# Two transposed weight loads of 640 rows issued as 512 and 128 rows each, with the waits split to match

## The chip, the core and the metric

The kernel runs on one core of one Trainium2 chip. The metric is the device time of one execution in microseconds (us); the span in a profile is some 1.3 us shorter.

## The reference, cut to what matters

Two branches over the same x (2048 x 640) are mixed by a gate.

```python
g = sigmoid((x * gate_w).sum(-1, keepdims=True))
# branch A: a diagonal complex state space model
Bu   = einsum("bld,pd->blp", x, B_bar)          # B_re and B_im, 640 x 640 each
hseq = scan(Lam_bar, Bu)
a    = 2 * einsum("blp,dp->bld", hseq, C).real + x * Dskip
# branch B: a dense layer pair, W1 640 x 1728, W2 1728 x 640
b    = gelu(x @ w1 + b1) @ w2 + b2
out  = g * a + (1 - g) * b
```

The kernel's matmuls take B_re and B_im transposed from SBUF (the on-chip memory), and it loads them with DMA transposes.

## The kernel before

The kernel is a list of operations with dependencies and priorities. A list scheduler in Python fixes each engine's order, and a wait is emitted for each dependency across engines. What matters here is the start. TensorE first multiplies the first quarter of x (512 tokens) by W1, in two parts. The first part (40 products, two of them split in halves) goes block by block as W1's row blocks arrive. The second part has 25 matmuls. Then come the 50 matmuls with B: 25 with B_re and 25 with B_im, five for each 128 rows of B.

```python
WSPLIT = {0: 4, 1: 6, 3: 6}          # W1's row blocks 0, 1 and 3 are loaded in two pieces
...
xtrans(0, range(4, 5), 4.5, 0.8)     # last number but one: priority on SyncE's queue
w1load(4, "sp", 5)                   # W1's fifth row block, 256 KB
...                                  # two more W1 loads (prio 20, 21)
for ci, src in enumerate((A_B_re, A_B_im)):
    load_T(f"B{ci}", f"l_B{ci}", [(BT[:, ci, :, :], src)], [("BT", ci)], prio=30 + ci, dur=4.1)
xtrans(1, range(KD), 32, 3.4)        # x, second quarter, a transpose too
load("gwb", "sp", "l_gwb", gwb[:, :], gate_w.partition_broadcast(128), ["gwb"], prio=32.2)
load("xnb", "sp", ...,     prio=32.4)                # both plain loads
...
def bproj(q):                        # the B product of quarter q
    for ci in range(2):
        for k in range(KP):          # KP = 5 blocks of 128 rows
            def f_mm(...):
                for kd in range(KD):
                    t = nc.tensor.matmul(PS[bank][:, :], BT[:, ci, kd, k * 128:(k + 1) * 128], xT[q][:, kd, :], ...)
            op(f"b_{q}_{k}{ci}", "pe", KD * d_mm(512), XT[q] + [("BT", ci)], [("bank", bank)], f_mm, prio=pe_prio())
```

All these loads are issued by SyncE, one after the other, on one queue. W1's first row block is already loaded in two halves (`WSPLIT`), here and in the changed kernel; the diff does not touch it.

Of the kernel before, what the change touches and what calls it, by code (L numbers as in the profile page):

```python
# [147 lines left out]
class Prog:  # L148
# [8 lines left out]
    def op(self, name, eng, dur, reads, writes, fn, prio=None, lat=0.0, after=()):  # L157
        deps = {}
        for k in reads:
            for w in self.last_w.get(k, ()):  # L160
                deps[w.idx] = w
        for k in writes:
            for w in self.last_w.get(k, ()):
                deps[w.idx] = w
            for r in self.last_r.get(k, ()):
                deps[r.idx] = r
        for a in after:
            deps[a.idx] = a
        deps = list(deps.values())
        E = self.E  # L170

        def run(eg, deps=deps, eng=eng, fn=fn):
            E.wait(eng, *[d.done for d in deps if not (eng == "pe" and d.eng == "pe")])
            return fn()

        it = self.sch.add(name, eng, dur, deps, run, prio=prio, lat=lat)
        for k in writes:
            self.last_w[k] = [it]
            self.last_r[k] = []
        for k in reads:  # L180
            self.last_r.setdefault(k, []).append(it)
        return it


def bass_gated_mix__ssm_conv_s5__dense_activation_gelu__prompt_kernel(
# [18 lines left out]
    _, S, D = A_x.shape  # L204
# [3 lines left out]
    KD = D // 128  # L208
    KP = P // 128
# [16 lines left out]
    with ExitStack() as es:  # L226

        def SB(name, shape, dt):
            return es.enter_context(nc.sbuf_tensor(name, list(shape), dt))
# [5 lines left out]
        BT = SB("BT", [128, 2, KD, P], BF16)  # L235
# [72 lines left out]
        op = pr.op  # L308

        def inc(eng, ins):  # L310
            return E.inc(eng, ins, eng + "_s")

        def dma_inc(eng, ins, sem):
            SEM(sem)
            E.count.setdefault(sem, 0)
            ins.then_inc(sems[sem], 16)
            E.count[sem] += 16
            return (sem, E.count[sem])

        def d_act(n):  # L320
            return 0.26 + n * 0.00084
# [4 lines left out]
        def d_mm(n):  # L326
            return n / 2400.0 + 0.004
# [8 lines left out]
        def load_T(name, sem, pairs, writes, prio, dur, lat=3.0, reads=()):  # L336
            def fn():
                t = None
                for dst, src in pairs:
                    t = dma_inc("sp", nc.sync.dma_start_transpose(dst, src), sem)  # L340
                return t
            return op(name, "sp", dur, reads, writes, fn, prio=prio, lat=lat)
# [10 lines left out]
        def xtrans(q, ks, prio, dur):  # L353
            load_T(f"xT{q}_{ks[0]}", f"l_xT{q}_{ks[0]}", [(xT[q][:, ks[0]:ks[-1] + 1, :], x2[q * 512:(q + 1) * 512, ks[0] * 128:(ks[-1] + 1) * 128])],
                   [("xT", q, k) for k in ks], prio, dur)
# [33 lines left out]
        for i, (nm, (r0, src)) in enumerate(ROWS.items()):  # L389
            src = src.rearrange("(k p) -> k p", p=128)  # L390
# [29 lines left out]
        for i, (k, c0, c1) in enumerate(((0, 0, 2), (0, 2, 4), (1, 0, 2), (1, 2, 4))):  # L420
            bank = (7, 6, 5, 4)[i]
# [18 lines left out]
        XT = {q: [("xT", q, k) for k in range(KD)] for q in range(1, NQ)}  # L440
# [137 lines left out]


        for ci, src in enumerate((A_B_re, A_B_im)):  # L580
            load_T(f"B{ci}", f"l_B{ci}", [(BT[:, ci, :, :], src)], [("BT", ci)], prio=30 + ci, dur=4.1)
        xtrans(1, range(KD), 32, 3.4)
        load("gwb", "sp", "l_gwb", gwb[:, :], gate_w.partition_broadcast(128), ["gwb"], prio=32.2)
        load("xnb", "sp", "l_xnb", xn[0][:, :, KN * 128:D], x2[0:512, KN * 128:D].rearrange("(c p) d -> p c d", p=128),
# [16 lines left out]
        def pe_prio():  # L601
            ctr["pe"] += 1
            return ctr["pe"]


        def next_bank():
            ctr["bank"] += 1
            return (ctr["bank"] - 1) % 8
# [87 lines left out]
        def bproj(q):  # L696
            for ci in range(2):
                for k in range(KP):
                    bank = next_bank()

                    def f_mm(k=k, ci=ci, bank=bank):
                        t = None
                        for kd in range(KD):
                            t = nc.tensor.matmul(PS[bank][:, :], BT[:, ci, kd, k * 128:(k + 1) * 128], xT[q][:, kd, :],  # L704
                                                 start=(kd == 0), stop=(kd == KD - 1))
                        return inc("pe", t)

                    op(f"b_{q}_{k}{ci}", "pe", KD * d_mm(512), XT[q] + [("BT", ci)], [("bank", bank)], f_mm, prio=pe_prio())

                    def f_ev(k=k, ci=ci, bank=bank):  # L710
                        dst = U[q % 2][:, :, ci, k, :]
                        src = PS[bank][:, :].rearrange("p (s t) -> p s t", s=2)
                        return inc("act", nc.scalar.activation(dst, src, ACT.Copy, scale=1.0 if ci == 0 else -1.0))  # L713

                    op(f"u_{q}_{k}{ci}", "act", d_act(512), [("bank", bank)], [("U", q % 2, k, ci)], f_ev, prio=10)
# [292 lines left out]
        m1_first()  # L1008
        m1(0, NW)
        bproj(0)  # L1010
        ssm(0)
        gates(0)
        m1(1)
        for q in range(0, NQ, 2):
            m1_tail(q)
        ssm(1)
        bproj(1)
        ssm(2)
        gates(1)
        outsT(0)  # L1020
        for q in range(2, NQ):
            ssm(2 * q - 1)
            bproj(q)
            ssm(2 * q)
            m1(q)
            xnload(q, "pool")
            gates(q)
            if q < NQ - 1:
                outsT(q - 1)
# [63 lines left out]
```

## Time and profile before

| | before |
|---|---|
| median of 3 runs | 213.42 us (213.19 to 213.48) |
| span of the profiled run | 212.1 us |
| TensorE busy | 208.9 us, 99% |
| first matmul with B | 19.72 us |
| from there to the end | 192.38 us |

The head of the page of the kernel before, and its section on the chain that ended last:

```profile
span 212.1 us, 2749 instructions
PE 208.9 (99%) x1102; PEld 104.9 (49%) x1102; DVE 190.2 (90%) x240; ACT 103.2 (49%) x177; POOL 4.2 (2%) x12
PE 90%; DMA 4%; SPq 4%; issue 0%; DVE 0%
```

TensorE has practically no idle time to give. The chain in order of time (start, duration, what) shows the only stretch of the chain that is a DMA:

```profile
9.87 0.53 SPq L333
10.39 0.04 issue
10.44 9.24 DMA BT<-in_A_B_re_dram
19.68 0.05 issue
19.72 10.97 PE ps L704 x50
30.69 14.03 PE ps L661 x65
```

From 19.72 us on, TensorE alone makes up the chain until 210.17 us. Before that the chain runs through SyncE's issues to B_re's load. The list of TensorE's waits (line, for what, us in total, times, longest) and the timelines of TensorE and of SyncE around that point:

```profile
PE ps L704 <- DMA BT<-in_A_B_re_dram: 0.4, 1, 0.4
```

```profile
13.79 5.56 PE L661 MATMUL ps<-xT,W1sb 128*128 128x512 bf16 x25
19.72 10.97 PE L704 MATMUL ps<-xT,BT 128*128 128x512 bf16 x50 [0.38 <-DMA BT<-in_A_B_re_dram]
```

```profile
10.44 5.35 SPq L340 DMA_TRANSPOSE BT<-in_A_B_re_dram  x1
15.82 4.61 SPq L340 DMA_TRANSPOSE BT<-in_A_B_im_dram  x1
20.48 3.32 SPq L340 DMA_TRANSPOSE xT<-in_A_x_dram  x1
```

The 0.38 us in brackets understates the loss, because a matmul's duration (379 ns) overlaps the next matmul: they start every 0.2155 us. The last W1 matmul started at 18.96 us, so the next could have started at 19.18. The start at 19.72 lost 0.54 us.

A DMA ends with up to sixteen completion events on its semaphore, one for each DMA engine; the Trainium skill says so in "DMA: Bandwidth & Descriptors", section "Why a DMA increments its semaphore by 16 and not by 1", and the trace agrees with sixteen events for each B load. B_re's came in two groups:

```
B_re, kernel before, completion events in us
17.65 17.66 17.68 17.71 17.77 17.80 | 19.56 19.58 19.60 19.61 19.61 19.62 19.62 19.64 19.66 19.68
```

### The profile page before, as it was taken

How to read it: one execution, taken by the hardware profiler on the slowest of the kernel's cores; microseconds unless marked ns; L12 is line 12 of the kernel's file. 1: busy time of each engine (PE TensorE's matmuls, PEld its weight loads, DVE VectorE, ACT ScalarE, POOL GpSimd, SP SyncE). 2: the span in 40 equal slices, each digit the busy share in tenths (PEclk: the TensorE clock that was granted, in tenths of full speed). 3: DMA queues.
4: the chain of work that ended last, by engine and by line, in shares of the span. 5: the costliest groups of instructions: out<-in, count | busy, mean ns of one | idle time of the engine just before them, and what ended most of it. 6: DMA issues, size and time to landing. Idle time of an engine off the chain costs nothing.

```text
span 212.1 us, 2749 instructions
## 1 busy us (share of the span) xinstructions
PE 208.9 (99%) x1102; PEld 104.9 (49%) x1102; DVE 190.2 (90%) x240; ACT 103.2 (49%) x177; POOL 4.2 (2%) x12
## 2 busy tenths in 40 slices
PE   8999999999999999999999999999999999999996
PEld 4443444444564444444464444444446444567775
DVE  2499999999999998999999999899999999499744
ACT  2488556679860253556681063455660027623330
POOL 1000000030000000000000000000010000000000
DMA  5899999998600020066363000007642000005251
GB/s 150 193 289 183 184 206 219 362 191 178 159 0 3 0 49 0 0 105 86 60 58 115 3 0 0 0 2 146 85 93 99 0 3 0 0 0 102 68 142 63
DMA packets 48888, 19.08 MB, mean 90 GB/s; under 512 B 41452, under 2 KB 47980, under 8 KB 48876
## 3 DMA queue, kind: packets, MB, share of 16 engines
q1 hardware_dynamic: 47216, 17.59, 39.7%
q0 software_dynamic: 1600, 1.32, 4.3%
q8 instruction: 8, 0.13, 0.3%
q14 instruction: 4, 0.03, 0.1%
q10 hardware_dynamic: 60, 0.01, 0.0%
HBM read 8.41 MB, written 2.63 MB: 52 GB/s over the span
## 4 chain that ended last, share of the span: by engine, by line
PE 90%; DMA 4%; SPq 4%; issue 0%; DVE 0%
PE ps L704 20%; PE ps L928 20%; PE ps L661 20%; PE ps L977 15%; PE ps L791 7%; PE ps L840 5%; DMA BT<-in_A_B_re_dram 4%; SPq L333 3%; SPq L340 2%; PE ps L682 1%; PE ps L939 1%; PE ps L805 0%; DVE W1sb L874 0%
## 5 line engine op out<-in xcount | busy, mean ns | idle before, releaser
L661 PE MATMUL ps<-xT,W1sb 128*128 128x512 bf16 x220 | 48.1, 379 | 0.0
L744 DVE TENSOR_TENSOR_SCAN W<-atab,V 128x1280 bf16<-128x1280 f32 x16 | 44.3, 2811 | 0.3
L704 PE MATMUL ps<-xT,BT 128*128 128x512 bf16 x200 | 43.8, 379 | 0.4 <-DMA BT<-in_A_B_re_dram 0.4
L928 PE MATMUL ps<-Gl,W2sb 128*128 128x512 bf16 (+1 forms) x234 | 42.7, 344 | 0.0
L668 ACT ACTIVATE Gl<-ps,cols 128x512 bf16<-128x512 f32 x44 | 29.9, 694 | 15.5 <-PE ps L661 15.5
L661 PEld LDWEIGHTS ps<-xT,W1sb 128*128 128x128 bf16 x220 | 21.5, 98 | 26.0
L977 PE MATMUL ps<-Hb,CT 128*128 128x512 bf16 x150 | 32.9, 379 | 0.0
L928 PEld LDWEIGHTS ps<-Gl,W2sb 128*128 128x128 bf16 x234 | 22.9, 98 | 19.3
L713 ACT ACTIVATE U<-ps 128x512 bf16<-128x512 f32 x40 | 23.7, 596 | 16.2 <-PE ps L704 16.1
L704 PEld LDWEIGHTS ps<-xT,BT 128*128 128x128 bf16 x200 | 19.4, 98 | 24.4 <-DMA BT<-in_A_B_re_dram 0.9
L946 ACT ACTIVATE E1T<-ps,cols 128x512 bf16<-128x512 f32 (+1 forms) x18 | 9.5, 624 | 36.0 <-PE ps L939 36.0
L977 PEld LDWEIGHTS ps<-Hb,CT 128*128 128x128 bf16 x150 | 14.4, 98 | 17.9 <-DVE V L496 0.6
L985 ACT ACTIVATE E2T<-ps 128x512 bf16<-128x512 f32 x15 | 9.1, 604 | 13.6 <-PE ps L977 13.6
L791 PE MATMUL ps<-W2sb,Gl 128*128 128x320 bf16 x104 | 14.8, 299 | 0.0
L614 DVE SCALAR_TENSOR_TENSOR trf<-xn,gwb 128x640 bf16<-128x640 bf16 x16 | 13.2, 823 | 0.4
L496 DVE TENSOR_TENSOR Hb<-Hb,V 128x1280 bf16<-128x1280 bf16 x16 | 12.5, 821 | 0.3
L496 DVE TENSOR_TENSOR V<-V,W 128x1280 bf16<-128x1280 bf16 x16 | 12.5, 821 | 0.3
L496 DVE TENSOR_TENSOR V<-mr,U 128x2560 bf16<-128x2560 bf16 x8 | 11.9, 1492 | 0.3
L791 PEld LDWEIGHTS ps<-W2sb,Gl 128*128 128x128 bf16 x104 | 10.1, 98 | 4.3 <-issue 0.3
L496 DVE TENSOR_TENSOR Hb<-c,W 128x2560 bf16<-128x2560 bf16 x8 | 11.9, 1491 | 0.2
L496 DVE TENSOR_TENSOR W<-mi,U 128x2560 bf16<-128x2560 bf16 x8 | 11.9, 1485 | 0.0
L496 DVE TENSOR_TENSOR V<-s,W 128x2560 bf16<-128x2560 bf16 x8 | 11.9, 1484 | 0.0
(91 smaller groups left out, 151.0 us busy)
## 6 DMA issues: line engine op xcount, KB each, us to landing
W2sb<-in_B_w_dram SPq DMA_DIRECT2D x1, 2080.0 KB, 8.7
out_dram<-xn SPq DMA_DIRECT2D x3, 640.0 KB, 4.8
xn<-in_A_x_dram POOLq DMA_DIRECT2D x2, 640.0 KB, 6.8
trf<-grow SPq DMA_DIRECT2D x3, 256.0 KB, 5.0
xn<-in_A_x_dram SPq DMA_DIRECT2D x1, 640.0 KB, 6.9
W1sb<-in_B_w_dram SPq DMA_DIRECT2D x2, 256.0 KB, 3.0
W1sb<-in_B_w_dram SPq DMA_DIRECT2D x1, 480.0 KB, 4.1
out_dram<-W1sb SPq DMA_DIRECT2D x3, 160.0 KB, 1.8
```

The source lines that it names most:

```text
L496: return inc("dve", nc.vector.tensor_tensor(out=o, in0=a, in1=b, op=o_))
L614: t = inc("dve", nc.vector.scalar_tensor_tensor(out=scr[:, :], in0=xn[q % 2][:, c, :], scalar=1.0, in1=gwb[:, :], op0=ALU.mult, op1=ALU.mu ...
L661: t = nc.tensor.matmul(PS[bank][:, :], W1sb[:, k, jf * 128:(jf + 1) * 128], xT[q][:, k, :], start=(k == 0), stop=(k == KD - 1))
L668: return inc("act", nc.scalar.activation(Gl[q % 2][:, jf, :], PS[bank][:, :], ACT.Gelu_apprx_tanh, bias=b1col[:, jf:jf + 1]))
L704: t = nc.tensor.matmul(PS[bank][:, :], BT[:, ci, kd, k * 128:(k + 1) * 128], xT[q][:, kd, :], start=(kd == 0), stop=(kd == KD - 1))
L713: return inc("act", nc.scalar.activation(dst, src, ACT.Copy, scale=1.0 if ci == 0 else -1.0))
L744: t = inc("dve", nc.vector.tensor_tensor_scan(out=g[:, ci, :], data0=a, data1=v[:, ci, :], initial=0.0, op0=ALU.mult, op1=ALU.add))
L791: t = nc.tensor.matmul(PS[bank][:, 0:HALF], Gl[q % 2][:, jf, t4 * 128:(t4 + 1) * 128], W2sb[:, jf, cols], start=False, stop=False, skip_gr ...
L840: t = nc.tensor.matmul(PS[bank][:, 0:n], H[b % NHB][:, ci, k, s * 128:(s + 1) * 128], CT[:, ci, k, cols], start=(i == 0), stop=(i == 2 * K ...
L928: t = nc.tensor.matmul(PS[bank][:, 0:t1 - t0], W2sb[:, jf, d * 128:(d + 1) * 128], Gl[q % 2][:, jf, t0:t1], start=(jf == 0), stop=False)
L946: return inc("act", nc.scalar.activation(E1T[:, d, t0:t1], PS[bank][:, 0:t1 - t0], ACT.Identity, bias=cols2[:, 0, d:d + 1]))
L977: t = nc.tensor.matmul(PS[bank][:, :].rearrange("p (s t) -> p s t", s=2), CT[:, ci, k, d * 128:(d + 1) * 128], Hb[:, 2 * (q % 2):2 * (q % ...
```

## The change

Each B matrix is loaded by two transposes, of 512 rows and of 128 rows. A B product waits only for the part that holds its own 128 rows. The intent is that TensorE can start on the first four row blocks of B_re before the fifth has landed.

```diff
         for ci, src in enumerate((A_B_re, A_B_im)):
-            load_T(f"B{ci}", f"l_B{ci}", [(BT[:, ci, :, :], src)], [("BT", ci)], prio=30 + ci, dur=4.1)
+            for i, (p0, p1) in enumerate(((0, 512), (512, KP * 128))):
+                load_T(f"B{ci}{i}", f"l_B{ci}{i}", [(BT[:, ci, :, p0:p1], src[p0:p1, :])], [("BT", ci, i)], prio=30 + ci + 0.1 * i, dur=0.8 * (p1 - p0) / 128)
...
-                    op(f"b_{q}_{k}{ci}", "pe", KD * d_mm(512), XT[q] + [("BT", ci)], [("bank", bank)], f_mm, prio=pe_prio())
+                    op(f"b_{q}_{k}{ci}", "pe", KD * d_mm(512), XT[q] + [("BT", ci, k // 4)], [("bank", bank)], f_mm, prio=pe_prio())
```

## The prediction

> **What bounds the kernel now.** The page gives TensorE 208.9 us busy of a 212.1 us span (99%). The chain of waits is TensorE at 90%, unbroken from 19.72 us to 210.17 us; ahead of it stand the first loads' issues and one 9.24 us DMA, the transposed load of B_re. The list of TensorE's waits names one on a DMA: 0.4 us for B_re. VectorE (190 us busy) has slack where TensorE needs it: its H for the output products at 72.5, 123.0 and 173.5 us was done at 67.8, 110.4 and 152.9 us.
>
> **The one spot the change touches.** In the timeline SyncE issues the B_re transpose from 10.44 to 15.79 us and B_im from 15.82 to 20.43. B_re's semaphore events in the trace: six of sixteen at 17.65-17.80 us, ten only at 19.56-19.68. TensorE starts its last matmul of the first W1 product at 18.97 us and its first B matmul at 19.72 us. Matmuls of this form follow each other every 0.216 us (50 in 10.79 us), so an unhindered start is 19.19 us: 0.53 us is lost. That is all a faster B_re can give; no engine work is removed.
>
> **What the change adds and moves.** Two transposes of 640 rows become four of 512, 128, 512, 128. Issue times in the trace: 3.32 us for 512x640 (x, second block), 1.12-1.20 us for 512x128. A line through these is about 0.57 us fixed plus 0.137 us per 128x128 block (an estimate): 3.3 + 1.3 = 4.6 us for a split matrix against 5.35 and 4.61 now. Landing ends 1.9 us after the issue ends when nothing delays it, up to 3.9 us with stragglers like B_re's.
> - B_re, 512 rows: issue ends at 13.8-14.8 us, landed at 15.7-18.7 us. Needed at 19.2: the wait goes.
> - B_re, 128 rows: needed 20 matmuls later, 23.5 us; landed by about 20.
> - B_im, 512 rows: landed at 20.3-23.4 us (now 23.12), needed at 24.6.
> - B_im, 128 rows: landed by 24.8, needed at 28.9.
> - x, second block: landed 25.8 us now, perhaps 26-28 then, needed at 30.2.
>
> Later loads have several us of slack.
> The kernel's list scheduler already assumes B there in time, so I expect no new instruction order.
>
> **The risk.** The destination of each transpose becomes strided (512 of 640 columns) where it was contiguous. The Trainium skill, "DMA: Bandwidth & Descriptors", section "Latency and other measured facts", gives 261 GB/s for a transpose with non-contiguous mid-dim against about 350-400 GB/s contiguous. This trace's contiguous ones move 290 GB/s in their bulk, so I expect little loss. And each hand-over from one transpose to the next shows a slow stretch (62-195 GB/s for 1 to 2 us behind B_re and B_im); two more of these could use up the roughly 1.3 us of margin of B_im.
>
> **Prediction.** 213.42 - 0.5 = 212.9 us; the gain is passed on whole because TensorE has no other wait. 80% range 212.5 to 213.5. Faster by over 2%: 0.01; within 2%: 0.97; slower by over 2%: 0.02.
>
> **What the profile would show.** Right: TensorE's 0.4 us wait for B_re gone, first B matmul near 19.2 us, the chain running on TensorE or its W1 loads before that, all later stages shifted by 0.4-0.5 us, unchanged busy times. Wrong: a B issue of 512 rows longer than 4.5 us, a wait of the 26th B matmul on B_im or of the second W1 product on x, or a later stage that doesn't shift since VectorE or a DMA holds it.

## The result, and the profile after

| | before | after |
|---|---|---|
| first measurement, median of 6 runs each | 213.50 us | 213.19 us |
| repeated later (after_again), median of 11 and 5 runs | 213.36 us | 213.05 us |
| span of the profiled run | 212.1 us | 211.7 us |
| last W1 matmul of the first quarter starts | 18.96 us | 19.11 us |
| first matmul with B starts | 19.72 us | 19.33 us |
| from there to the end | 192.38 us | 192.38 us |

The ratio to before was 0.9987 (95% interval 0.9974 to 1.0000), and 0.9980 (0.9963 to 0.9996) in the repetition. A ratio is the mean time of one kernel's runs over that of the other's of the same rounds, so it is not quite the ratio of the medians quoted here. The change is worth 0.1 to 0.2%. The first interval touches 1 and the repetition's stays below it.

The head of the page of the changed kernel and its chain by engine:

```profile
span 211.7 us, 2739 instructions
PE 207.5 (98%) x1088; PEld 104.7 (49%) x1102; DVE 190.1 (90%) x240; ACT 103.0 (49%) x177; POOL 4.2 (2%) x12
PE 93%; SPq 4%; DMA 2%; issue 1%; DVE 0%
```

The lower busy time of TensorE is not less work. The page counts 1,088 matmuls where 1,102 weight loads are recorded: fourteen matmul records are missing from this trace, and some short "issue" gaps of TensorE in it are those holes. The chain in order of time around the start, changed kernel:

```profile
8.77 3.30 DMA W1sb<-in_B_w_dram
12.07 0.14 issue
12.21 1.89 PE ps L640 x8
14.09 5.40 PE ps L662 x25
19.49 3.45 PE ps L705 x16
```

B_re is gone from the chain. What stands there now is the load of W1's fifth row block. The waits of TensorE and the timelines say the same:

```profile
PE ps L640 <- DMA W1sb<-in_B_w_dram: 0.6, 1, 0.6
```

```profile
12.21 1.89 PE L640 MATMUL ps<-xT,W1sb 128*128 128x512 bf16 x8 [0.62 <-DMA W1sb<-in_B_w_dram]
13.93 5.56 PE L662 MATMUL ps<-xT,W1sb 128*128 128x512 bf16 x25
19.33 10.96 PE L705 MATMUL ps<-xT,BT 128*128 128x512 bf16 x49
```

```profile
10.44 6.26 SPq L340 DMA_TRANSPOSE BT<-in_A_B_re_dram  x2
16.74 4.85 SPq L340 DMA_TRANSPOSE BT<-in_A_B_im_dram  x2
21.63 2.92 SPq L340 DMA_TRANSPOSE xT<-in_A_x_dram  x1
```

From 13.93 us the timeline has no bracket: TensorE goes from W1 to B without standing still. The span shrank by 0.4 us, which is the 0.54 us no longer lost at B minus 0.15 us by which the W1 part ended later in this execution. Instruction order on all compute engines is the same as before.

The order of events of the four parts, from the semaphore events (last of sixteen): B_re 512 rows 17.83 us, B_re 128 rows 20.23, B_im 512 rows 22.73, B_im 128 rows 24.03, x second quarter 26.60.

### The profile page after: what moved, and what is told of

Read it like the earlier page. It is cut to its first block, busy times and chain, and to the rows that moved or that the text cites. A ratio compares the mean times of both kernels' runs of the same rounds, so it can differ in the third digit from the quotient of the medians.

```text
span 211.7 us, 2739 instructions
## 1 busy us (share of the span) xinstructions
PE 207.5 (98%) x1088; PEld 104.7 (49%) x1102; DVE 190.1 (90%) x240; ACT 103.0 (49%) x177; POOL 4.2 (2%) x12
## 4 chain that ended last, share of the span: by engine, by line
PE 93%; SPq 4%; DMA 2%; issue 1%; DVE 0%
PE ps L662 22%; PE ps L705 20%; PE ps L929 20%; PE ps L978 15%; PE ps L792 7%; PE ps L841 5%; SPq L333 2%; SPq L340 2%; DMA W1sb<-in_B_w_dram 2%; PE ps L683 1%; PE ps L940 1%; PE ps L640 1%; PE ps L806 0%; DVE W1sb L875 0%
## 5 line engine op out<-in xcount | busy, mean ns | idle before, releaser
L662 PE MATMUL ps<-xT,W1sb 128*128 128x512 bf16 x215 | 47.5, 379 | 0.3
L705 PE MATMUL ps<-xT,BT 128*128 128x512 bf16 x196 | 43.1, 379 | 0.3 <-issue 0.2
L929 PEld LDWEIGHTS ps<-Gl,W2sb 128*128 128x128 bf16 x234 | 22.9, 98 | 19.3
L705 PEld LDWEIGHTS ps<-xT,BT 128*128 128x128 bf16 x200 | 19.5, 98 | 23.8 <-ACT Gt L691 0.4
```

The costliest lines, as they stand in the source:

```text
L662: t = nc.tensor.matmul(PS[bank][:, :], W1sb[:, k, jf * 128:(jf + 1) * 128], xT[q][:, k, :], start=(k == 0), stop=(k == KD - 1))
L929: t = nc.tensor.matmul(PS[bank][:, 0:t1 - t0], W2sb[:, jf, d * 128:(d + 1) * 128], Gl[q % 2][:, jf, t0:t1], start=(jf == 0), stop=False)
```

## The experiments

The explanation read from the two profiles (theory A) is: only the earlier landing of B_re's first rows matters, the transfers are no faster, and afterwards the early W1 loads set the pace. The traces bear out the middle part: all of B_re had landed at 19.68 us before, and only at 20.23 and 19.88 us in the two profiles of the change. Two rivals for *why* the whole B_re landed so late came up as well. Theory H: a second transpose right behind on the same queue holds up the landing. Theory F: a 16 KB instruction fetch, which starts at 17.05 us in the kernel before, holds it up.

"Lost" below is the start of the first B matmul minus that of the last W1 matmul minus 0.2155 us. Span minus first B start is 192.36 to 192.41 us in every profile but those of e6 and e9 (193.01 and 192.71), where B_im comes late. So apart from these, **the start of the first B matmul alone decides the time**. By the same rule a run without a profile tells roughly where its first B matmul started, by its span less 192.37 us: an estimate of 19.1 to 19.9 us over the eleven runs of the change, and 19.4 to 20.6 us over the eleven of the kernel before in the repetition. One profile is one draw from such a range.

| kernel | last W1 mm | first B mm | lost | span | ratio to before (95%) |
|---|---|---|---|---|---|
| before | 18.96 | 19.72 | 0.54 | 212.1 | 1 |
| the change | 19.11 | 19.33 | 0 | 211.7 | 0.9987 (0.9974-1.0000) |
| after_again | 18.95 | 19.16 | 0 | 211.5 | 0.9980 (0.9963-0.9996) |
| e1_re_only | 18.94 | 19.45 | 0.29 | 211.9 | 0.9980 (0.9966-0.9994) |
| e2_wait_both | 19.21 | 20.16 | 0.73 | 212.5 | 0.9998 (0.9978-1.0018) |
| e3_before_fetch | 20.36 | 20.58 | 0 | 212.9 | 1.0037 (1.0021-1.0054) |
| e4_after_w14 | 19.97 | 20.19 | 0 | 212.6 | 0.9990 (0.9973-1.0007) |
| e5_before_w14 | 20.24 | 20.71 | 0.25 | 213.1 | 1.0036 (1.0016-1.0056) |
| e6_before_gap | 19.14 | 19.36 | 0 | 212.4 | 1.0018 (0.9999-1.0037) |
| e7_after_fetch | 20.25 | 20.46 | 0 | 212.8 | 1.0037 (1.0021-1.0053) |
| e8_after_w4split | 19.34 | 19.56 | 0 | 211.9 | 1.0001 (0.9985-1.0017) |
| e9_before_gwb | 19.15 | 19.36 | 0 | 212.1 | 0.9980 (0.9965-0.9995) |
| e10_after_gwb | 19.22 | 19.44 | 0 | 211.8 | 0.9979 (0.9966-0.9992) |
| e11_after_gwb_w4split | 19.20 | 19.42 | 0 | 211.8 | 0.9982 (0.9969-0.9995) |

The profile columns are from one execution each; the ratios are from 5 or 6 timed runs against 6 (the first measurement of the change) or 11 (all others) of the kernel before. All outputs were correct.

### after_again: the change once more

The edit adds nothing. It gives a second profile and more timings.

> The change unaltered, for a second profile and more timings. Ratio 0.997 to 0.9998. If the early W1 loads set its time, the first B matmul starts 0.22 us after the last W1 matmul starts unless the instruction fetch falls into the landing of B_re's first part, in which case it lands near 19.4-20 us and up to 0.5 us are lost again.

Measured: ratio 0.9980, 0 lost. TensorE goes through from W1 to B:

```profile
13.77 5.56 PE L662 MATMUL ps<-xT,W1sb 128*128 128x512 bf16 x25
19.16 10.96 PE L705 MATMUL ps<-xT,BT 128*128 128x512 bf16 x49
```

In this execution there was no wait for W1's fifth block either, so that wait comes and goes.

### e1_re_only: split B_re alone

```diff
-            for i, (p0, p1) in enumerate(((0, 512), (512, KP * 128))):
+            for i, (p0, p1) in enumerate(((0, 512), (512, KP * 128)) if ci == 0 else ((0, KP * 128),)):
...
-    XT[q] + [("BT", ci, k // 4)]
+    XT[q] + [("BT", ci, k // 4 if ci == 0 else 0)]
```

> Only B_re is split in 512 and 128 rows, B_im stays whole. Theory A (the gain is the earlier landing of B_re's first 512 rows alone): B_re's 512 rows land near 17.8 us, TensorE has no wait for B_re, first B matmul near 19.1 us, time like the change's: ratio to before 0.997 to 0.9995. Rival: the split of B_im is needed too, then a wait on B_im appears at the 26th B matmul and the ratio is 0.9995 or more.

Measured: ratio 0.9980, as with the full change: splitting B_im contributes nothing that shows. The profile was worse than expected, though:

```profile
13.76 5.57 PE L662 MATMUL ps<-xT,W1sb 128*128 128x512 bf16 x25
19.45 10.75 PE L705 MATMUL ps<-xT,BT 128*128 128x512 bf16 x49
```

B_re's first 512 rows landed only at 19.40 us, in two groups again, and 0.29 us were lost. B_im landed at 24.76 us, just in time: the weight load of the 26th B matmul started 0.16 us late, but the matmul itself, at 24.86 us, did not. So an early landing of the first part is not assured; the table further below shows when it fails. Even here something was gained: the landing took 3.9 us from the end of the issue, as in the kernel before, but the issue of 512 rows ended 0.28 us sooner than that of 640.

### e2_wait_both: the four transposes, but each product waits for both parts

```diff
-    XT[q] + [("BT", ci, k // 4)]
+    XT[q] + [("BT", ci, 0), ("BT", ci, 1)]
```

> The same four transposes as in the change, but every B product waits for both parts of its matrix. Theory A (the gain is the finer wait, the transfers are no faster): both parts of B_re are there only at about 20.2 us, first B matmul near 20.3 us, about 1.1 us later than with the change and 0.5 us later than before: ratio 1.002 to 1.005. Rival B (four smaller transposes are faster as transfers): no worse than before, ratio 0.9985 to 1.000.

Measured: both parts were there at 20.07 us and the first B matmul started at 20.16, as theory A had it. (The view names "issue" as what ended the wait; the landing is read from the semaphore events.) The last W1 line and the B line of this kernel's timeline:

```profile
14.04 5.56 PE L662 MATMUL ps<-xT,W1sb 128*128 128x512 bf16 x25
20.16 10.09 PE L705 MATMUL ps<-xT,BT 128*128 128x512 bf16 x46 [0.56 <-issue]
```

The ratio, 0.9998 (0.9978 to 1.0018), missed the 1.002 or more expected under theory A and lies in the range given for rival B. It cannot separate the theories: the runs scattered from 212.82 to 214.14 us, the interval also holds the change's 0.9980, and the profiled run was the second slowest of six. By the estimate from spans the fastest run started B at 19.1 us, without a wait. What speaks for theory A is the traces: with the same four transposes and coarse waits, 0.73 us were lost in this profile; with fine waits, none in the two of the change; and all of B_re landed later than before in all three (20.07, 20.23 and 19.88 us). The gain comes from the finer wait, not from faster transfers; how much a coarse wait costs on average these runs do not tell.

### e4_after_w14 and e5_before_w14: W1's fifth block issued earlier

If the W1 loads now set the pace, issuing the late one sooner should help the changed kernel and not the old one. The same edit on the change (e4) and on the kernel before (e5):

```diff
-        w1load(4, "sp", 5)
+        w1load(4, "sp", 4.4)      # ahead of the fifth x transpose (4.5)
```

> The change, and W1's fifth row block is issued ahead of the fifth x transpose instead of behind it. Theory A (with the change the W1 loads, not B, set when the B product starts): the wait of 0.6 us on that block goes, it lands near 10.5 us instead of 12.07, first B matmul near 18.5 us, ratio 0.995 to 0.998. Rival: the B product's start is bound by B_re at 17.8 us or by another early load, no more gain: ratio 0.9985 to 0.9995.

> The kernel before with the same swap of two issues, transposes whole. Theory A: B_re still lands at about 19.7 us, so the first B matmul stays at 19.7 us and the wait for B_re only grows to 0.8-1.2 us: ratio 0.9990 to 1.0010. Rival: the swap is worth as much here as on top of the change, ratio 0.995 to 0.998.

Measured: theory A failed in both. For e4 its rival came true: another early load takes over, ratio 0.9990. For e5 neither range held, since the kernel became slower. The fifth block stopped being late, but the next W1 load, now right behind a transpose, landed at 14.73 us (e4) and 15.01 us (e5) instead of 13.45, and TensorE waited for that one. The start of the second part of the W1 product, e4 first, then e5:

```profile
14.78 5.57 PE L662 MATMUL ps<-xT,W1sb 128*128 128x512 bf16 x25 [1.19 <-DMA W1sb<-in_B_w_dram]
```

```profile
15.06 5.57 PE L661 MATMUL ps<-xT,W1sb 128*128 128x512 bf16 x25 [0.98 <-DMA W1sb<-in_B_w_dram]
```

The swap made the kernel before 0.36% slower; on top of the change it left no gain over before that clears the noise. It moved the wait rather than removing it, and it confirms in the other direction that a later W1 part delays everything behind it.

### e3_before_fetch and e7_after_fetch: 84 instructions more in TensorE's queue

The trace shows eight DMA packets of 16,384 bytes on the instruction queue. The Trainium skill, "Runtime: NRT & Kernel Launch", section "Instruction fetch mechanics", says that a sequencer refills its instruction memory in blocks of 16 KiB, 256 instructions, over a DMA queue of its own. That fits TensorE: the trace lists 2,228 instructions for it (1,102 matmuls, 1,102 weight loads, 24 others), which make 8.7 such blocks. To move the fetch, waits that are already satisfied were put in (the same edit on both kernels). Four for each of 42 matmuls are 168 calls; the traces list 84 more instructions, and nine fetches instead of eight:

```diff
                 def f_mm(jf=jf, k=k, t0=t0, t1=t1):
+                    for _ in range(4):
+                        nc.tensor.wait_ge(sems["pe_s"], 1)
                     return inc("pe", nc.tensor.matmul(...))   # first part of the W1 product
```

> The kernel before, with four waits that are always satisfied ahead of each of the first 42 W1 matmuls (84 more instructions in TensorE's queue), nothing else. In five profiles out of six a 16 KB instruction fetch starts at 16.9 to 18.4 us, and B_re's or its first part's last engines land 1.1 to 1.9 us after the first ones. Theory F (the fetch, TensorE's own, holds B_re up): 84 instructions more bring the fetch forward by some 5 us, to about 11-12 us; B_re lands 1.9 to 2.5 us after its issue ends, so at 17.7-18.3 us instead of 19.7; TensorE's wait for B_re goes, ratio 0.997 to 0.9995 without any split. Theory H (the next transpose, right behind, holds it up): B_re still lands at 19.5-19.9 us, ratio 0.9995 to 1.001. If the extra instructions slow TensorE, the gaps between its first 42 matmuls grow beyond 0.216 us.

> The change, with the same 84 satisfied waits as the other run. Theory F: the first 512 rows of B_re land at 17.3-18 us in this profile too, TensorE doesn't wait for them; the split has then nothing more to give than the moved fetch: ratio to before 0.997 to 0.9995, within 0.1% of the kernel before with the moved fetch. Rival: the split and the moved fetch add up, ratio 0.994 to 0.997.

Measured: the extra instructions cost TensorE 1.3 to 1.4 us in the first part of W1 (its second part starts at 15.19 and 15.07 us, against 13.79), so the times cannot test theory F. Neither ratio, 1.0037 twice, lies in a range that was expected. Two things can still be read. First, the second and third fetches came earlier, 46.29 to 38.62 us and 66.80 to 60.39 us, so they are TensorE's; the first did not move (17.47 us in e3, 1.3 us after the end of B_re's issue, as before). It seems to be held back until a transpose has been read; that was not tested. In e3 B_re landed in two groups again, at 19.70 us.

Second, e3 and e7 are a clean test of the explanation. Here TensorE comes to B at 20.5 us, after B_re's landing (19.70 us whole in e3, 18.72 us for the first part in e7), and the two kernels, one split and one not, have the same ratio, 1.0037. **Where B is not waited for, the split is worth nothing.** The B line of e3, without a wait, and its two B issues:

```profile
20.59 9.66 PE L706 MATMUL ps<-xT,BT 128*128 128x512 bf16 x43
```

```profile
10.43 5.74 SPq L340 DMA_TRANSPOSE BT<-in_A_B_re_dram  x1
16.21 4.08 SPq L340 DMA_TRANSPOSE BT<-in_A_B_im_dram  x1
```

### e6_before_gap and e9_before_gwb: no split, plain loads between the two transposes

e6 moves two plain loads between the whole transposes of B_re and B_im, e9 only the gate row (160 KB):

```diff
-    load("gwb", ..., prio=32.2)
+    load("gwb", ..., prio=30.2)        # e6 and e9
-    load("xnb", ..., prio=32.4)
+    load("xnb", ..., prio=30.4)        # e6 alone
```

> The kernel before, with two plain loads (the gate row and the rest of x's first block) moved between the two B transposes. Theory H: with no transpose right behind it B_re lands within 2.4 us of its issue's end, at 17.7-18.2 us, the wait for it goes: ratio 0.997 to 0.9995 if B_im, about 1 us later, is still in time (24.6 us). Theory F: the fetch at about 17 us still holds B_re up to 19.3-19.9 us: ratio 0.9995 to 1.002.

> The kernel before, with one plain load alone (the gate row, 160 KB) between the whole transposes of B_re and B_im. Theory H (a transpose right behind holds the landing up, a plain load doesn't): B_re lands in one group within 2.4 us of its issue's end, by 18.3 us, TensorE loses nothing at the first B matmul; B_im is some 0.6-1 us later than before, 23.7-24.7 us, and may or may not be in time at 24.5 us: ratio 0.997 to 1.000. If H is wrong, B_re lands at 19.4-19.9 us and 0.2-0.7 us are lost at the first B matmul.

Measured: in both, B_re landed in a single group, at 17.97 us (e6) and 18.07 us (e9), although a fetch began at 17.29 and 17.49 us in the middle of it. So theory F alone falls, and the transpose right behind, as theory H has it, is needed for the late landing. (e6's ratio, 1.0018, is what theory F gave, but for another reason: the wait for B_im below.) The two times from issue to landing of the B loads (last number, us), of the kernel before, then of e9:

```profile
BT<-in_A_B_re_dram SPq DMA_TRANSPOSE x1, 9.2
BT<-in_A_B_im_dram SPq DMA_TRANSPOSE x1, 7.3
```

```profile
BT<-in_A_B_re_dram SPq DMA_TRANSPOSE x1, 7.6
BT<-in_A_B_im_dram SPq DMA_TRANSPOSE x1, 8.3
```

B_re landed 1.6 us sooner, but B_im was issued later and took 1.0 us longer, so it landed at 25.05 us instead of 23.12. Nothing is lost any more at the first B matmul, but B_im comes late at the 26th. The timelines of e6 and of e9:

```profile
19.36 5.56 PE L704 MATMUL ps<-xT,BT 128*128 128x512 bf16 x24
25.39 4.92 PE L704 MATMUL ps<-xT,BT 128*128 128x512 bf16 x22 [0.47 <-DMA BT<-in_A_B_im_dram]
```

```profile
19.36 5.56 PE L704 MATMUL ps<-xT,BT 128*128 128x512 bf16 x25
25.10 5.14 PE L704 MATMUL ps<-xT,BT 128*128 128x512 bf16 x23 [0.18 <-DMA BT<-in_A_B_im_dram]
```

With two loads between, the wait for B_im eats the gain (1.0018). With the small one alone the kernel is as good as the change (0.9980) by moving one line and splitting nothing. One rival stays untested: the plain load also puts the next transpose's issue 0.67 us (e9) or 1.14 us (e6) after the end of B_re's, against 0.04 us before. Whether it is the plain load or the pause that helps, these runs do not separate.

### e8_after_w4split, e10_after_gwb, e11_after_gwb_w4split: attempts to go further

```diff
-        WSPLIT = {0: 4, 1: 6, 3: 6}
+        WSPLIT = {0: 4, 1: 6, 3: 6, 4: 4}      # e8 and e11: the fifth W1 block in two halves
-    load("gwb", ..., prio=32.2)
+    load("gwb", ..., prio=30.05)               # e10 and e11: the gate row between B_re's two parts
```

> The change, and W1's fifth row block is loaded in two halves too (one more load issue of about 0.45 us ahead of B_re). With the change TensorE is bound by the W1 loads up to 19.1-19.3 us; in one of its two profiles it stood still 0.75 us for this block at 12.2 us. If that wait is typical, the first half lands by 11.4 us, the second W1 product starts at 13.5-13.8 us, the first B matmul at 18.9-19.2 us: ratio to before 0.9955 to 0.998. If the wait is rare or moves to the next load: like the change, 0.998 to 0.9995.

> The change, with the gate row's load between B_re's two parts. Theory H: B_re's 512 rows land in one group by 17.8 us whether or not an instruction fetch falls there, nothing is lost at the first B matmul; B_im's 512 rows still land by 24.0 us: ratio like the change's, 0.997 to 0.9995. If B_im's part comes after 24.4 us, a wait shows at the 26th B matmul.

> Both additions on top of the change. The best that I expect: no wait for B, W1's fifth block in time, first B matmul at 18.9-19.2 us, ratio 0.9955 to 0.998; no better than the change (0.998 to 0.9995) if the W1 wait is rare.

Measured: halving the fifth W1 block gave nothing (1.0001 in e8, worse than either range that was expected). In e8's profile TensorE waited earlier on, at 5.9 to 6.6 us, and the second part started at 14.17 us; in e11 the wait moved to the next W1 load (0.46 us). With the gate row behind B_re's first part (e10, e11) that part landed in one group, at 17.18 and 17.47 us, and nothing was lost, but TensorE was not waiting for it with the plain change either. Ratios of 0.9979 and 0.9982 cannot be told from the change's. No version beat both kernels clearly.

### What the fourteen landings show together

For each profile: the end of the issue of B_re (of its first part, where split), the time from there to its last completion event, and the start of the first fetch counted from there. All in us, worked out from the traces.

```
what is right behind it   fetch inside   issue end to last event      kernels
transpose                 yes            3.53 3.53 3.55 3.77 3.89 3.89  e3 e5 e7 e4 e1 before
transpose                 no *           2.27 2.36 2.43 2.45            e8 after_again e2 after
plain load                yes            1.99 2.00 2.00                 e6 e9 e11
plain load                no             2.03                           e10
* first fetch 2.33 us or more after the issue's end, so only when all or nearly all had landed
```

In the nine cases "inside" the fetch starts 1.27 to 1.42 us after the issue's end. The first column was changed on purpose (e6, e9, e10, e11), so it is shown that what is queued right behind decides: with a fetch inside, 2.0 us behind a plain load and 3.5 to 3.9 us behind a transpose. Without a fetch the transpose adds only 0.2 to 0.4 us, judged against the one profile of e10. The second column was never moved on purpose. That a fetch adds another 1.1 to 1.6 us when, and only when, a transpose follows is a regularity of fourteen profiles without an exception, not a proven cause. The other B transposes of the same traces, all with a transpose right behind, fit it: B_re's second part took 3.3 to 4.3 us with a fetch inside (seven profiles) and 2.8 and 1.6 us without (e2, e11), and B_im or its parts, never with a fetch, 2.3 to 3.1 us. In the kernel before, the DMA engines together moved only 6 to 9 GB/s from 18.5 to 19.5 us, just ahead of the second group of events; what held them is not known.

Splitting lets the first part end its issue sooner, at 15.3 us, and then the fetch sometimes comes in behind the second part and not the first. So it was in the two profiles of the change; in e1, e4 and e7 the fetch hit the first part. Which it will be is open.

## Why the prediction was right

- **Which stage and which wait.** Right. The only thing lost was the wait for B_re, 0.53 us by the prediction, 0.54 by the finer reading. It went, and the time after the first B matmul is 192.38 us before and after. "TensorE has no other wait" did not hold in the first profile of the change: 0.62 us went to W1's fifth block.
- **The size.** Predicted 212.9 us within 212.5 to 213.5, measured 213.19 us, and 213.05 us in the repetition. The range also holds the 213.42 us of no change at all, so the hit says little; the profile says more. The gain was 0.3 us by the medians of both measurements instead of 0.5. The prediction took TensorE's arrival at B as fixed at 19.19 us. It is not: over the eight profiles with unchanged W1 loads and no added instructions (before, the change, after_again, e1, e2, e6, e9, e10) the last W1 matmul starts between 18.94 and 19.22 us, on average 19.09 us, so TensorE could start B at 19.30 on average. Against 19.72 that is a gain of about 0.4 us, if B_re is always in time, and e1 shows that it isn't.
- **Issue times.** Wrong. The straight line through the x transposes gave 3.3 us, and 3.4 to 4.4 us were allowed, for 512 rows of B_re; it took 4.94 us (10.44 to 15.38). The prediction named over 4.5 us as a sign of error. The 128-row part took 1.28 us as predicted, and B_im's 512 rows 3.52 us. W1 loads were still landing while B_re was issued (until 15.0 us); that this makes the issue longer is argued, not tested. It did no harm because the landing, 17.83 us, was still inside the 15.7 to 18.7 us that the prediction gave. That was partly luck: the issue ended 0.6 us after the latest end that the prediction allowed, and with the 3.9 us that it allowed for stragglers the landing would have been at 19.3 us (an estimate), about when TensorE got there. In e1 it was so.
- **The other parts in time.** Right: B_re's rest at 20.23 us (needed at 23.5), B_im at 22.73 and 24.03 us, x at 26.60 us (needed at 30.2).
- **The strided destination.** The feared loss did not come. The bulk of B_re's first part moved at 285 to 294 GB/s in the two profiles of the change, against 288 to 293 with the contiguous destination before (transposed bytes in each quarter of a microsecond from 15.25 us on). The figure quoted from the Trainium skill, 261 GB/s for a non-contiguous middle dimension, did not bind here, if this destination is what the page means.
- **The hand-over from one transpose to the next.** The prediction saw the slow stretch and feared it for B_im. It belongs rather to the late B_re: without a transpose right behind, the landing took 2.0 us instead of 3.9.

## What to carry to other kernels

When an engine waits for one load, first find out how much later than needed the load is, and whether all of its engines are late or only some: here ten of sixteen completion events came 1.8 us after the others. A plain load between two transposes on one queue can be worth as much as splitting the first transpose, and costs one line. And the gain of removing a wait ends at the next arrival: here that was the early W1 loads, whose scatter from profile to profile moved TensorE's arrival at B by 0.28 us, nearly the whole gain.

## What the Trainium skill lacked or had wrong

- "DMA: Bandwidth & Descriptors", section "Rules for kernel authors", says that a transpose next to ordinary DMAs needs nothing, and orders transposes of different queues. It has nothing on the time of two transposes back to back on one queue: B_re (or its first part) landed 2.3 to 3.9 us after its issue ended, against 2.0 us with a plain load right behind it.
- "Runtime: NRT & Kernel Launch", section "Instruction fetch mechanics", calls the cost of crossing a 16 KiB block mostly hidden. The fetch's packets took 0.9 to 1.6 us around B_re, and in all six profiles in which one fell into the landing of a transpose with another behind it, the landing took 3.5 to 3.9 us, against 2.3 to 2.45 us in the four without. That is a coincidence seen, not a cause shown. The section doesn't mention that fetches and loads can meet.
- "DMA: Bandwidth & Descriptors", section "Latency and other measured facts": 261 GB/s for a transpose with non-contiguous middle dimension against about 350 to 400 contiguous. Here the bulk moved at 288 to 293 GB/s contiguous, below the page's contiguous figure, and at 285 to 294 strided: no difference. Only if a strided destination is what the page means does this contradict it.
